# A windowed-attention and top-1 expert kernel: its late expert passes put into the order of the source

## The chip, the cores and the metric

The kernel runs on one core of one Trainium2 chip. The metric is the device time of one execution in microseconds (us), the median of the runs shown. Engines are named as in the profile: PE is TensorE (matmuls; PEld its weight loads), DVE VectorE, ACT ScalarE, POOL GpSimd, SP SyncE, whose queue issues most of the DMAs.

## What is computed

```python
# attention, B=8, H=8, S=576, D=64, causal window of 64
scores = q @ k.T / 8, masked to 0 <= rel < 64
x = softmax(scores) @ v                 # laid out as 4608 rows of 512
# top-1 mixture of 8 experts, D=512, F=1024
logits = x @ w_gate ; e = argmax ; gate = softmax(logits)[e]
out[row] = gate * (relu(x[row] @ w1[e]) @ w2[e])
```

## The kernel before

**Three stages.** A long loop over 36 steps (lines 859 to 932) does the attention of 128 rows a step, stores them in DRAM as `xs` and sorts the rows by expert. In its last steps and after it, four *early* passes (`first_passes`, L822) each take 256 rows of experts 0 to 3. Then `chain` (L967) runs 15 *late* passes: pass 0 and 1 are *wide* (three blocks of 128 rows), passes 2 to 14 are *narrow* (two blocks). Passes beyond these stand behind conditions (L987 to L1000) that do not hold for this input.

**One pass** is `expert` (L290), which walks over eight *slices* j of the 1024 hidden columns. A slice is: the split of the next slice's weights (`split_`, L228: ACT rounds the loaded `raw` to `whi`, L241, DVE forms the rest `wlo`, L238), twelve *up* matmuls into a PSUM bank `hp` (L308 with `whi`, L312 with `wlo`), ACT's `hh` (L318) and DVE's `hl` (L319) from that bank, and then the *down* matmuls of the slice before (`flush`, L279: three a block, of 512 columns), which collect in the banks `yp`. The down matmuls of a pass's slice 7 thus come behind the up matmuls of slice 0 of the next pass. After a pass's last down matmuls ACT scales the rows (`ys`, L267) and POOL scatters them to `out` (L268).

**The weights** of an expert come in four loads of 1 MB (`load`, L210), into the three buffers of `raw`. A split for slices 2r and 2r+1 needs load r; the code asks for load r+1 at the split of slice 2r at the latest. `open_weights` (L812) reads the next pass's expert number into a register of SP and asks for load 0.

**The rows of the next pass** are fetched by POOL (`get`, L774, one indirect DMA a block into one of three buffers `xg`). Pass 0 and the early passes turn them on PE (`turn`, L187: four transposes, an ACT copy L193, a DVE subtraction L194). For passes 1 to 14 four steps do it for each block u: `part` (L786) has DVE separate the two 16-bit halves of each number into `planes` (L790; two buffers) and SP issue a DMA transpose into `halves` (L793; three buffers); `join` (L795) has ACT put the halves together (L799); `lay` (L802) has ACT (L809) and DVE (L810) make the rounded part `xh` and the rest `xl`.

**What sets the order.** Each engine and SP's queue work in order. Within `tc.manual_schedule()` (L857 to L964: the attention and the early passes) the order on each engine is that in which the source issues the instructions. `chain` at L984 stands outside of it: there a planner that estimates costs chooses the order, and it may place instructions of the chain among those of the early passes, as soon as it holds their inputs and buffers to be ready. In the source, `chain` asks for `get(i+2)` after slice 2, `open_weights(i+1)` after slice 4, and for `part`, `join` and `lay` of block u after slices u, 3+u and 4+u.

**The banks.** `turns["yp"]` holds the two halves of one tile `x_b` and two tiles `e_b`, taken in rotation; `t_b` and `m_b` serve `turn`.

Of the kernel before, what the change touches and what calls it, by code (L numbers as in the profile page):

```python
# [14 lines left out]
U16 = mybir.dt.uint16  # L15
# [7 lines left out]
C = H * D  # L23
E, F = 8, 1024
N = B * S
P = 128
# [4 lines left out]
NJ = F // P  # L31
# [16 lines left out]
WIDE = 3  # L48
NWIDE = 2
NARROW = (N // P + E - 1 + E) // 2  # L50
ALWAYS = 13
# [68 lines left out]
def window_attention_then_top1_moe(ctx: ExitStack, tc: tile.TileContext, qkv, wall, wg, cst, out):  # L120
# [13 lines left out]
    t_b = ps.tile([P, C], F32, name="t_b")  # L134
    m_b = ps.tile([P, C], F32, name="m_b")
# [4 lines left out]
    turns = {}  # L140

    def bank(name):

        turns[name].append(turns[name].pop(0))
        return turns[name][-1]
# [38 lines left out]
    def columns(pool, nu=WIDE):  # L184
        return tuple(pool.tile([P, 4, nu * P], F32R, name=n) for n in ("xh", "xl"))
# [12 lines left out]
    class Weights:  # L198


        def __init__(self, ev, spread=0):
            self.ev, self.loaded, self.given, self.raws = ev, 0, 0, {}
            self.first, self.ready, self.spread = None, deque(), spread
            self.load()
# [23 lines left out]
        def split_(self, pieces=None, lows=None):  # L228
            jj, r = divmod(self.given, 2)
            self.given += 1  # L230
            while self.loaded < min(jj + 2, NJ // 2):
                self.load()
            hi = ws.tile([P, 2 * C], F32R, name="whi")
            lo = ws.tile([P, 2 * C], F32R, name="wlo")
            raw = self.raws[jj][:, r]

            def low(s=slice(0, 2 * C)):
                nc.vector.tensor_tensor(out=lo[:, s], in0=raw[:, s], in1=hi[:, s], op=ALU.subtract)  # L238

            def piece(s):  # L240
                nc.scalar.copy(out=hi[:, s], in_=raw[:, s])  # L241
                low(s)

            if lows is not None:
                nc.scalar.copy(out=hi, in_=raw)
                lows.append(low)
            elif pieces is None:
                piece(slice(0, 2 * C))
            else:
                w = 2 * C // 4  # L250
                pieces.extend(lambda s=slice(k * w, (k + 1) * w): piece(s) for k in range(4))
            return hi, lo

    def expert_of(m):
        return nc.sync.value_load(es_sb[m:m + 1, 0:1], min_val=0, max_val=E - 1)
# [3 lines left out]
    def flush(final=False):  # L259

        if not late:
            return
        (hh, hl), yp, (hi, lo), j, last = late.pop()
        def finish(u):
            ix, gate = last[0][u], last[1][u]
            ys = hw.tile([P, C], F32, name="ys")
            nc.scalar.activation(out=ys, in_=yp[u], func=AF.Copy, scale=gate)  # L267
            ins = nc.gpsimd.indirect_dma_start(  # L268
                out=out, out_offset=bass.IndirectOffsetOnAxis(ap=ix, axis=0), in_=ys, in_offset=None,
                bounds_check=N - 1, oob_is_err=False)  # L270

            for o in outs:
                tc.declare_no_dep(ins.ins, o.ins, reason="scatters to rows of their own")
            outs.append(ins)

        for u, y in enumerate(yp):
            us = slice(u * P, (u + 1) * P)
            for m, (x, w) in enumerate(((hh, hi), (hh, lo), (hl, hi))):
                nc.tensor.matmul(y, lhsT=x[:, us], rhs=w[:, C:], start=(j == 0 and m == 0),  # L279
                                 stop=(j == NJ - 1 and m == 2))  # L280
            if final:
                finish(u)
            if u + 1 < len(yp):
                yield
        if last is not None and not final:
            for u in range(len(yp)):
                finish(u)
        yield

    def expert(xt, idx, gates, wts, following=None):  # L290


        xh, xl = xt
        nu = len(idx)
        w = nu * P
        yp = None
        cur = wts.first
        for j in range(NJ):
            if j + 1 < NJ:
                nxt = wts.split()  # L300
            elif following is not None:
                following().first = following().split()
            hi, lo = cur
            hp = bank("hp")
            for kk in range(4):
                ks = slice(kk * P, (kk + 1) * P)
                for x in (xh, xl):
                    nc.tensor.matmul(hp[:, 0:w], lhsT=hi[:, ks], rhs=x[:, kk, 0:w], start=(kk == 0 and x is xh), stop=False)  # L308
                if kk & 1:
                    yield  # L310
            for kk in range(4):
                nc.tensor.matmul(hp[:, 0:w], lhsT=lo[:, kk * P:(kk + 1) * P], rhs=xh[:, kk, 0:w], start=False,  # L312
                                 stop=(kk == 3))
                if kk == 1:
                    yield
            hh = hw.tile([P, WIDE * P], F32R, name="hh")
            hl = hw.tile([P, WIDE * P], F32R, name="hl")
            nc.scalar.activation(out=hh[:, 0:w], in_=hp[:, 0:w], func=AF.Relu)  # L318
            nc.vector.scalar_tensor_tensor(out=hl[:, 0:w], in0=hp[:, 0:w], scalar=0.0, in1=hh[:, 0:w],  # L319
                                           op0=ALU.max, op1=ALU.subtract)  # L320
            yield
            yield from flush()
            if yp is None:
                yp = [bank("yp") for u in range(nu)]
            late.append(((hh, hl), yp, cur, j, (idx, gates) if j == NJ - 1 else None))
            cur = nxt
            yield j
# [439 lines left out]
    passes = [range(WIDE * t, WIDE * (t + 1)) for t in range(NWIDE)]  # L767
    passes += [range(m, m + 2) for m in range(WIDE * NWIDE, NM, 2)]
    xt, wts = {}, {}

    def cols(t, ms):
        return [t[:, m:m + 1] for m in ms]

    def get(i):  # L774
        fetch(xg[i % 3], cols(idx_sb, passes[i]))
# [8 lines left out]
    halves, joined = {}, {}  # L784

    def part(i, u):  # L786
        if u >= len(passes[i]):
            return
        pl = xq.tile([P, 2, C], U16, name="planes")
        nc.vector.tensor_copy(out=pl, in_=xg[i % 3][:, u].bitcast(U16).rearrange("p (f s) -> p s f", s=2))  # L790
        src = pl.rearrange("p s f -> p (s f)")
        halves[i, u] = xq.tile([P, 2 * 4, P], U16, name="halves", bufs=3)
        nc.sync.dma_start_transpose(out=halves[i, u], in_=src)  # L793

    def join(i, u):  # L795
        if u >= len(passes[i]):
            return
        x = joined[i, u] = xq.tile([P, 4, P], F32, name="joined", bufs=3)
        nc.scalar.copy(out=x.rearrange("p k t -> p (k t)").bitcast(U16).rearrange("p (t s) -> p s t", s=2),  # L799
                       in_=halves.pop((i, u)).rearrange("p (s k) t -> p s (k t)", s=2))  # L800

    def lay(i, u):  # L802
        if u >= len(passes[i]):
            return
        if u == 0:
            xt[i] = columns(xw)
        x, us = joined.pop((i, u)), slice(u * P, (u + 1) * P)
        xh, xl = xt[i]
        nc.scalar.copy(out=xh[:, :, us], in_=x)  # L809
        nc.vector.tensor_tensor(out=xl[:, :, us], in0=x, in1=xh[:, :, us], op=ALU.subtract)  # L810

    def open_weights(i):  # L812
        wts[i] = Weights(expert_of(passes[i][0]))

    def each(f, n):
        if 0 <= n < NS:
# [40 lines left out]
    with tc.manual_schedule():  # L857
        keep_busy(BUSY[0])
        for i in range(NS + LAST):
# [36 lines left out]
            if slow and slow[0][0]:  # L896
                f = slow.popleft()[1]
# [41 lines left out]
        xq = ctx.enter_context(tc.tile_pool(name="xq", bufs=2))  # L939
# [27 lines left out]
    def chain(first, last):  # L967
        for i in range(first, last):
            fol = (lambda i=i: wts[i + 1]) if i + 1 < last else None
            for j in expert(xt.pop(i), cols(idx_sb, passes[i]), cols(gate_sb, passes[i]), wts.pop(i), fol):  # L970
                if j == 2 and i + 2 < last:
                    get(i + 2)
                if j == 4 and i + 1 < last:
                    open_weights(i + 1)
                if j in (0, 1, 2) and i + 1 < last:
                    part(i + 1, j)
                if j in (3, 4, 5) and i + 1 < last:
                    join(i + 1, j - 3)
                if j in (4, 5, 6) and i + 1 < last:
                    lay(i + 1, j - 4)  # L980
        for _ in flush(True):
            pass

    chain(0, NWIDE + ALWAYS)  # L984
    total = nc.values_load(tot_sb[0:1, 0:1], min_val=0, max_val=NARROW)
    more = ExitStack()
    for lo, hi in zip(TAIL, TAIL[1:] + [NARROW]):  # L987
# [44 lines left out]
```

## Time and profile before

| what | value |
|---|---|
| median of 3 runs | 654.26 us (653.3 to 655.69) |
| the profiled execution, its own time | 659.39 us |
| its span, first to last instruction | 657.6 us |
| PE busy | 603.9 us (92%) |
| DVE, ACT, POOL busy | 414.4, 391.9, 200.5 us |
| granted TensorE clock, mean | 0.985 of full speed |

The profile page gives busy times by engine, the granted clock and the load of the DMA engines by fortieths of the span, and the chain of work that ended last. Beside it the trace answers questions on a stretch: which instructions ran on an engine, how long the engine sat idle before each (in square brackets, with what ended the idle time), and how busy each engine was. Busy time of PE is no measure of work done at full speed; the granted clock stands beside it.

### The profile page before, as it was taken

To read this page: it belongs to the slowest core of one execution; us is meant where nothing else is said; L and a number is where in the kernel's file an instruction comes from. 1 tells how busy PE (TensorE), PEld (TensorE's weight loads), DVE (VectorE), ACT (ScalarE), POOL (GpSimd) and SP (SyncE) were. 2 spreads that over 40 slices of the span, in tenths; PEclk is the share of its full clock that TensorE was granted. 3 is DMA by queue.
4 is the path that set the end of the run, shared out by engine and by line. 5 is a ranking of instruction groups with operands and counts; after the bars stand their busy time and mean duration, and the time that the engine had idled before them with its cause. 6 is when DMAs were issued, how large, how long until landed. Compare 5 with 4: busy or idle time off the path is not lost.

```text
span 657.6 us, 16869 instructions
## 1 busy us (share of the span) xinstructions
PE 603.9 (92%) x6879; PEld 533.0 (81%) x6879; DVE 414.4 (63%) x736; ACT 391.9 (60%) x792; POOL 200.5 (30%) x180
## 2 busy tenths in 40 slices
PE   8788998788989986995999999999999999999995
PEld 4677877677868975794998889899999999999994
DVE  3666778885699543754454666766666756665551
ACT  4576677675444444661636577667756775776551
POOL 4666667586240343232121232133101110110011
PEclk9999999999999999896999999999999999999999
DMA  8978888843744669797555687788667776565620
GB/s 301 346 257 273 285 262 297 288 154 138 240 152 176 245 224 212 233 218 162 171 193 164 253 261 199 274 278 258 221 219 255 230 235 222 209 215 192 224 98 34
DMA packets 65735, 145.74 MB, mean 222 GB/s; under 512 B 35564, under 2 KB 36716, under 8 KB 56176
## 3 DMA queue, kind: packets, MB, share of 16 engines
q1 hardware_dynamic: 59248, 125.68, 59.2%
q0 software_dynamic: 6400, 18.88, 9.0%
q8 instruction: 56, 0.92, 0.6%
q14 instruction: 31, 0.25, 0.1%
HBM read 119.11 MB, written 19.92 MB: 211 GB/s over the span
## 4 chain that ended last, share of the span: by engine, by line
PE 45%; issue 8%; DMA 6%; DVE 2%; ACT 2%; POOL 1%; POOLq 0%; DVEq 0%; ACTq 0%
PE e_b L308 15%; PE x_b L279 11%; PE e_b L279 11%; PE e_b L312 8%; DMA halves<-planes 5%; DVE wlo L238 1%; DMA xg<-xs,idx_sb 1%; ACT whi L241 1%; POOL out L268 1%; DVE planes L790 1%; ACT joined L799 0%; DVE hl L319 0%; ACT xh L809 0%; ACT ys L267 0%; ACT hh L318 0%
## 5 line engine op out<-in xcount | busy, mean ns | idle before, releaser
L238 DVE TENSOR_TENSOR wlo<-raw,whi 128x1024 fp32r<-128x1024 f32 (+1 forms) x158 | 187.3, 1191 | 102.2 <-ACT whi L241 98.5
L241 ACT CAST whi<-raw 128x1024 fp32r<-128x1024 f32 (+1 forms) x153 | 154.6, 1019 | 97.0 <-PE x_b L279 49.2
L308 PE MATMUL e_b<-xh,whi 128*128 128x256 f32 (+1 forms) x480 | 125.7, 290 | 0.1
L308 PE MATMUL e_b<-xl,whi 128*128 128x256 f32 (+1 forms) x480 | 125.8, 291 | 0.0
L268 POOL DMA_INDIRECT out<-ys,idx_sb x32 | 35.8, 1118 | 280.9 <-ACT ys L267 274.1
L445 POOL TENSOR_TENSOR pm<-tsb,cs 128x512 f32<-128x512 f32 x72 | 90.3, 1275 | 53.1 <-ACT tsb L438 44.9
L318 ACT ACTIVATE hh<-e_b 128x256 fp32r<-128x256 f32 (+1 forms) x152 | 60.3, 397 | 75.1 <-PE e_b L312 72.4
L308 PEld LDWEIGHTS e_b<-xh,whi 128*128 128x128 f32 x480 | 91.3, 190 | 5.3 <-ACT xh L193 0.6
L308 PEld LDWEIGHTS e_b<-xl,whi 128*128 128x128 f32 x480 | 91.2, 190 | 4.9 <-DVE xl L194 0.3
L319 DVE SCALAR_TENSOR_TENSOR hl<-e_b,hh 128x256 fp32r<-128x256 f32 (+1 forms) x152 | 65.8, 433 | 37.4 <-ACT hh L318 35.1
L312 PE MATMUL e_b<-xh,wlo 128*128 128x256 f32 (+1 forms) x480 | 79.9, 288 | 0.0
L279 PE MATMUL e_b<-whi,hl 128*128 128x512 f32 x160 | 63.8, 399 | 11.3 <-DVE hl L319 11.3
L429 ACT ACTIVATE pf<-s_b,mxs 128x64 f32<-128x64 f32 x288 | 62.9, 338 | 10.8 <-DVE mxs L421 8.0
L312 PEld LDWEIGHTS e_b<-xh,wlo 128*128 128x128 f32 x480 | 67.8, 188 | 0.2 <-DVE wlo L238 0.2
L180 POOL DMA_INDIRECT xg<-xs,idx_sb x32 | 42.9, 1342 | 81.7 <-DVE planes L790 33.1
L279 PE MATMUL x_b<-whi,hh 128*128 128x512 f32 x160 | 63.7, 398 | 0.8 <-ACT ys L267 0.8
L459 PE MATMUL x_b<-ring,pm 64*64 64x65 f32 x2176 | 47.0, 222 | 18.7 <-issue 10.8
L279 PE MATMUL x_b<-whi,hl 128*128 128x512 f32 x160 | 63.6, 398 | 0.3 <-DVE hl L319 0.2
L279 PE MATMUL x_b<-wlo,hh 128*128 128x512 f32 x160 | 63.6, 397 | 0.0
L279 PE MATMUL e_b<-wlo,hh 128*128 128x512 f32 x160 | 63.1, 394 | 0.0
L279 PE MATMUL e_b<-whi,hh 128*128 128x512 f32 x160 | 63.0, 394 | 0.0
L459 PEld LDWEIGHTS x_b<-ring,pm 64*64 64x64 f32 x2176 | 41.6, 134 | 24.5 <-issue 16.4
(164 smaller groups left out, 914.4 us busy)
## 6 DMA issues: line engine op xcount, KB each, us to landing
raw<-wall SPq DMA_DIRECT2D x74, 1024.0 KB
ring<-qkv SPq DMA_DIRECT2D x66, 386.0 KB
xs<-xrow SPq DMA_DIRECT2D x36, 256.0 KB
raw<-wall SPq DMA_DIRECT2D x8, 256.0 KB
ring<-qkv SPq DMA_DIRECT2D x4, 256.0 KB
ring<-qkv SPq DMA_DIRECT2D x4, 130.0 KB
ring<-qkv SPq DMA_DIRECT2D x1, 512.0 KB
xg<-xs,idx_sb POOLq DMA_INDIRECT x32
```

The source lines that it names most:

```text
L180: nc.gpsimd.indirect_dma_start(out=t[:, u], out_offset=None, in_=xs[0:rows], in_offset=bass.IndirectOffsetOnAxis(ap=ix, axis=0), bounds_ch ...
L238: nc.vector.tensor_tensor(out=lo[:, s], in0=raw[:, s], in1=hi[:, s], op=ALU.subtract)
L241: nc.scalar.copy(out=hi[:, s], in_=raw[:, s])
L268: ins = nc.gpsimd.indirect_dma_start(out=out, out_offset=bass.IndirectOffsetOnAxis(ap=ix, axis=0), in_=ys, in_offset=None, bounds_check=N ...
L279: nc.tensor.matmul(y, lhsT=x[:, us], rhs=w[:, C:], start=(j == 0 and m == 0), stop=(j == NJ - 1 and m == 2))
L308: nc.tensor.matmul(hp[:, 0:w], lhsT=hi[:, ks], rhs=x[:, kk, 0:w], start=(kk == 0 and x is xh), stop=False)
L312: nc.tensor.matmul(hp[:, 0:w], lhsT=lo[:, kk * P:(kk + 1) * P], rhs=xh[:, kk, 0:w], start=False, stop=(kk == 3))
L318: nc.scalar.activation(out=hh[:, 0:w], in_=hp[:, 0:w], func=AF.Relu)
L319: nc.vector.scalar_tensor_tensor(out=hl[:, 0:w], in0=hp[:, 0:w], scalar=0.0, in1=hh[:, 0:w], op0=ALU.max, op1=ALU.subtract)
L429: nc.scalar.activation(out=pf[:, g, a], in_=sp[:, a, g, 0], func=AF.Exp, bias=mx[:, h:h + 1], scale=SCALE)
L445: nc.gpsimd.tensor_tensor(out=pm[i], in0=t.rearrange("p (g q) -> p g q", g=NG), op=ALU.mult, in1=cc("mask")[:, i * P:(i + 1) * P].unsqueez ...
L459: nc.tensor.matmul(x_b[cols, a, g * V1:(g + 1) * V1], lhsT=pm[i][rows, g, cols], rhs=v_r[rows, c % RING - i, g], start=(i == 0), stop=(i = ...
```

## The change

`chain(0, 15)` moves into a `tc.manual_schedule()` of its own, so that the late passes run in the order of the source. In that order, `part` of the next pass's block u stands after slice u, `join` after slice 3+u (wide pass running) or 4+u (narrow pass running), `lay` one slice behind `join`. `planes` has three buffers instead of two. `open_weights` stands after slice 3 instead of 4, further loads are asked for after slices 4 and 6, and with `far` the split of an odd slice asks for one load more. The last pass takes `t_b` and `m_b` as its banks `yp`.

```diff
-        def __init__(self, ev, spread=0):
+        def __init__(self, ev, spread=0, far=False):
+            self.far = far
...
+            if self.far and r and self.loaded < min(jj + 3, NJ // 2):
+                self.load()
             return hi, lo
...
-        pl = xq.tile([P, 2, C], U16, name="planes")
+        pl = xq.tile([P, 2, C], U16, name="planes", bufs=3)
...
     def open_weights(i):
-        wts[i] = Weights(expert_of(passes[i][0]))
+        wts[i] = Weights(expert_of(passes[i][0]), far=True)
...
     def chain(first, last):
         for i in range(first, last):
             fol = (lambda i=i: wts[i + 1]) if i + 1 < last else None
+            if i + 1 == last:
+                turns["yp"] = [t_b, m_b]
+            gap = 3 if len(passes[i]) == WIDE else 4
             for j in expert(xt.pop(i), cols(idx_sb, passes[i]), cols(gate_sb, passes[i]), wts.pop(i), fol):
+                if j is None or i + 1 == last:
+                    continue
                 if j == 2 and i + 2 < last:
                     get(i + 2)
-                if j == 4 and i + 1 < last:
+                if j == 3:
                     open_weights(i + 1)
-                if j in (0, 1, 2) and i + 1 < last:
-                    part(i + 1, j)
-                if j in (3, 4, 5) and i + 1 < last:
-                    join(i + 1, j - 3)
-                if j in (4, 5, 6) and i + 1 < last:
-                    lay(i + 1, j - 4)
+                if j in (4, 6):
+                    wts[i + 1].load()
+                for f, at in ((part, 0), (join, gap), (lay, gap + 1)):
+                    if 0 <= j - at < len(passes[i + 1]):
+                        f(i + 1, j - at)
         for _ in flush(True):
             pass
 
-    chain(0, NWIDE + ALWAYS)
+    with tc.manual_schedule():
+        chain(0, NWIDE + ALWAYS)
```

## Rows read from the trace of the kernel before

**Rows 1.** Busy time by stretch: window, length, each engine (instructions), clock, DMA share, GB/s.

```profile
241.30:279.60 38.30, 28.22 (x162) 24.00 (x160) 19.58 (x28) 19.99 (x30) 11.10 (x9) 0.91 0.86 228
279.60:321.70 42.10, 34.30 (x161) 30.59 (x162) 19.96 (x26) 16.86 (x23) 10.73 (x8) 0.88 0.77 175
321.70:355.00 33.30, 33.30 (x171) 30.14 (x169) 16.67 (x21) 17.27 (x24) 6.10 (x5) 1.00 0.56 183
355.00:625.80 270.80, 270.42 (x1733) 245.38 (x1732) 173.43 (x231) 183.13 (x260) 43.44 (x35) 1.00 0.71 233
```

**Rows 2.** Waits of PE from 241 to 322: total us, times, longest.

```profile
PE e_b L279 <- DVE hl L319: 10.4, 2, 7.8
PE e_b L312 <- DVE wlo L238: 5.7, 2, 3.1
```

**Rows 3.** Chain that ended last, 225 to 312: start, us, what.

```profile
249.69 12.74 DMA halves<-planes
...
288.29 13.81 DMA halves<-planes
```

**Rows 4.** DVE in order of time: start, us, instruction, idle time before it.

```profile
244.83 0.69 DVE L790 COPY planes<-xg 128x1024 uint16<-128x1024 uint16 x1 [4.74 <-DMA xg<-xs,idx_sb]
...
262.53 0.69 DVE L790 COPY planes<-xg 128x1024 uint16<-128x1024 uint16 x1 [7.29 <-DMA halves<-planes]
```

**Rows 5.** PE in order of time: first up matmul of passes, one down matmul.

```profile
217.56 0.39 PE L279 MATMUL x_b<-whi,hl 128*128 128x512 f32 x1
217.79 0.28 PE L308 MATMUL e_b<-xeh,whi 128*128 128x256 f32 x1
...
241.26 0.28 PE L308 MATMUL e_b<-xeh,whi 128*128 128x256 f32 x1
...
279.62 0.44 PE L308 MATMUL e_b<-xh,whi 128*128 128x384 f32 x1
...
321.55 0.34 PE L308 MATMUL e_b<-xh,whi 128*128 128x384 f32 x1
...
354.88 0.28 PE L308 MATMUL e_b<-xh,whi 128*128 128x256 f32 x1
...
625.75 0.28 PE L308 MATMUL e_b<-xh,whi 128*128 128x256 f32 x1
```

**Rows 6.** All engines in order of time around one block turned on PE.

```profile
271.21 0.60 PE L191 MATMUL m_b<-cs,xg 128*128 128x128 f32 x4
271.57 0.36 PE L308 MATMUL e_b<-xeh,whi 128*128 128x256 f32 x1
...
272.46 0.69 DVE L194 TENSOR_TENSOR xl<-m_b,xh 128x512 fp32r<-128x512 f32 x1 [1.61 <-ACT xh L193]
```

**Rows 7.** Chain that ended last, whole span: start, us, what.

```profile
403.91 4.57 DMA halves<-planes
...
452.31 0.95 PE e_b L308 x8
...
474.71 0.95 PE e_b L308 x8
```

**Rows 8.** Groups from 290 on: count, busy us, mean ns, idle us before.

```profile
L241 ACT CAST whi<-raw 128x1024 fp32r<-128x1024 f32 x115 | 120.0, 1054 | 92.7 <-PE x_b L279 49.2 <-PE e_b L279 41.0 <-DMA raw<-wall 1.2
...
L318 ACT ACTIVATE hh<-e_b 128x256 fp32r<-128x256 f32 x104 | 40.1, 386 | 30.9 <-PE e_b L312 30.4 <-issue 0.4
...
L799 ACT COPY joined<-halves 128x1024 uint16<-128x1024 uint16 x23 | 31.3, 1362 | 0.5 <-DVE xl L810 0.5
...
L809 ACT CAST xh<-joined 128x512 fp32r<-128x512 f32 x26 | 14.7, 618 | 0.0
```

**Rows 9.** All engines in order of time at the end of the kernel.

```profile
649.77 0.50 PE L279 MATMUL x_b<-whi,hh 128*128 128x512 f32 x1 [0.78 <-ACT ys L267]
...
649.99 0.98 POOL L268 DMA_INDIRECT out<-ys,idx_sb  x1 [18.68 <-ACT ys L267]
...
651.74 0.98 POOL L268 DMA_INDIRECT out<-ys,idx_sb  x1 [0.77 <-ACT ys L267]
```

More of the change, by code (lines that the diff above doesn't have):

```diff
@@ L786, in part @@
     def part(i, u):
-        if u >= len(passes[i]):
-            return
-        pl = xq.tile([P, 2, C], U16, name="planes")
+        pl = xq.tile([P, 2, C], U16, name="planes", bufs=3)
         nc.vector.tensor_copy(out=pl, in_=xg[i % 3][:, u].bitcast(U16).rearrange("p (f s) -> p s f", s=2))
@@ L795, in join @@
     def join(i, u):
-        if u >= len(passes[i]):
-            return
         x = joined[i, u] = xq.tile([P, 4, P], F32, name="joined", bufs=3)
@@ L802, in lay @@
     def lay(i, u):
-        if u >= len(passes[i]):
-            return
         if u == 0:
```

## The prediction

> **What bounds the kernel now.** I read first where PE, the busiest engine, is not busy in the late part, then what it waits for there, then the engine that it waits for. The table of stretches [rows 1] splits the late part at the starts of passes. From 355.0 to 625.8 us (twelve narrow passes) PE is busy for 270.42 of 270.80 us at full clock; the wide pass 1 before it, 321.7 to 355.0, has no idle time at all. There nothing but fewer matmuls would help. The two stretches ahead are different: 28.22 busy of 38.30 us in the last early pass, 34.30 of 42.10 in late pass 0, and the granted clock is 0.91 and 0.88 on average, so at the lower of its two levels (1.2 instead of 2.4 GHz) for part of both. So the loss is local: it lies between 241 and 322 us.
>
> PE's waits there [rows 2] are for DVE: 10.4 us for `hl`, 5.7 us for `wlo`. These two are short instructions; the question is what DVE did instead. DVE's own order [rows 4] shows it: a `planes` copy of 0.69 us stands idle 4.74 us at 244.83, until the fetched rows land, and another 7.29 us until 262.53, for a DMA transpose to free one of two `planes` buffers. `planes` belongs to the chain, yet 244.83 lies in the last early pass, which begins at 241.26 and ends with the first up matmul of pass 0 at 279.62 [rows 5]. So the planner outside of the manual region has put work of the next pass into DVE's in-order queue ahead of work that PE needs at once. The chain of waits says the same: two transposes of 12.74 and 13.81 us stand on it [rows 3]. In the steady part the one long transpose of the chain took 4.57 us [rows 7].
>
> **Part 1: the order of the source, 241 to 322 us.** With the chain in a manual region, no `part` can come ahead of the early passes' instructions on DVE, nor a `join` on ACT. What the stretch should then take comes from neighbours that run without such work. The early pass before (217.79 to 241.26) took 23.47 us with two blocks turned; the last one turns three, and a turn takes PE 0.36 us (271.21 to 271.57) [rows 6]: 23.83 us. Wide pass 1 took 33.33 us (321.55 to 354.88) [rows 5]; pass 0 is like it, but its first down matmuls are those of a two-block pass, six instead of nine at 0.23 us (217.56 to 217.79): 32.64 us. Together 56.5 us, against 80.3 us (241.26 to 321.55): 23.8 us to gain, some 14.5 in the early pass (38.36 less 23.83) and 9.3 in pass 0.
>
> The new order also costs something here. The third block of pass 0 is turned behind the last slice of the early pass, and in the source the next PE instruction is the up matmul that needs the result; the six down matmuls that could hide it come later. From the start of a turn to the end of DVE's `xl` it was 1.94 us (271.21 to 273.15), of which PE works 0.36 [rows 6]. So up to 1.6 us of stall, nothing if a planner-like overlap remained; the source leaves none, so I take 1.5. Net 22.3 us.
>
> **Part 2: the steady passes.** PE cannot go faster, so the question is whether the new order holds it up. ACT has 1.05 for `whi` and 0.39 for `hh` in each slice, and in the fullest slice of a narrow pass also a `join` of 1.36 and an `xh` of 0.62 [rows 8]: 3.42 us against a slice of 2.80 us (22.40 from pass to pass, 452.31 to 474.71, by eight) [rows 7]. The slices around it need 2.80 and 2.06, so the excess of 0.6 is made up in the next one, and the hidden part is possible because a slice's down matmuls come behind the next slice's up matmuls, 2.8 us after `hh` can start. I cost it at nothing; without that cover it would be 0.6 us a narrow pass, 8 us in all. The two scaled outputs `ys` come at a slice without `join` and are left where they are. What can still be gained: 270.87 us (354.88 to 625.75) stand against 12 times 22.40 and 0.69 for the first pass's wide down matmuls, 269.5. Between 0 and 1.4 us; the traces name no cause that the change removes, so 0.
>
> **Part 3: DMAs and SP's queue.** Moved with the order are the transposes (3 for pass 1, 2 for each later pass), the fetches and the weight loads. A transpose now is issued behind slice u and needed four narrow slices later, 11.2 us (12.5 in a wide pass). The steady one took 4.57 us, so it is hidden, and the third `planes` buffer takes away the wait of DVE seen in [rows 4]. In SP's queue the load asked for after slice 2's split stands behind the second transpose, and the loads after slices 3, 4 and 6 wait for buffers whose last readers are splits already issued; behind each waits only the next load or transpose. ACT waited 1.2 us in all for a weight load in the passes from 290 on [rows 8], which is the only sign of a late load. Cost between 0 and 1.2 us a narrow pass, nearest to 0 because SP was that far ahead before; 0 taken. The register read in `open_weights` moves one slice earlier on SP alone: nothing.
>
> On the transposes a rule stands against the first part. The row: 12.74 and 13.81 us where fetches were issued beside them, 4.57 in the steady stretch [rows 3, 7]. The Trainium skill ("DMA: Bandwidth & Descriptors", section "Queues, rings and completion order") says that each DMA engine takes turns, packet by packet, between the queue rows that have work, so a transpose beside a fetch is slow wherever the source puts it. By that rule pass 0, which has three transposes, the scatters of the early pass and the fetch of pass 2, could keep its loss; that is the second rival below.
>
> **Part 4: the last pass's banks.** Its last three down matmuls stood idle 0.78 us for `ys` of the other half of the same tile [rows 9]; with separate tiles they do not. POOL issues the second scatter at 651.74, and the first keeps it to 650.97, so at most 0.77 us reach the end; I take 0.5. Nothing else of the tail moves.
>
> **The sum.** 22.3 + 0 + 0 + 0.5 = 22.8 us; with all bounds on the good side 25.7 (23.8 + 1.4 + 0.5), and 17 if loads or ACT's order take a few us. The profiled execution took 659.39 us, 5.1 more than the median of 654.26. On the profiled one the sum gives 636.6, on the median 631.5. If those 5.1 us lie in the very transposes that go (tracing may slow them), the median gains only 17.7 and the time is 636.5; that end stays in the range.
>
> **Rivals.**
> *Slower: late transposes stall ACT in every pass.* ACT works in order, so a `join` whose transpose has not landed holds up `whi` and `hh`. The new order issues transposes later than the planner did. At 13.81 us [rows 3] one is 2.6 us late against 11.2, and ACT has no slack to hide it (part 2), so 13 narrow passes lose 34 us, the sum turns to a loss of 11 and the time to 665. It decides from 22.8 over 13, 1.75 us a pass, that is from transposes of 13.0 us. For it: two of that length were seen. Against it: in the steady stretch scatters ran beside them as well and the chain has 4.57. The Trainium skill ("DMA: Bandwidth & Descriptors", "Rules for kernel authors") advises to issue a DMA early and to wait for it late, which speaks for this rival; the row of 4.57 does not bear it out.
>
> *Only half: pass 0 keeps its loss.* Its transposes have 12.5 us; if they take 13 to 14 and the slices pile up as before, the 9.3 us stay and the gain is 14.5 − 1.5 + 0.5 = 13.5: 640.8.
>
> *Weights late.* The odd load behind the transposes costs ACT 1.2 us in each of 13 passes, 15.6: gain 7, time 647.
>
> *No change.* The loss moves on: the rows for pass 1 come from the same fetches, and the transposes still meet the loads; PE waits as long, only later. 654. Against it: the queue order, not the DMA, made PE wait in [rows 4].
>
> **How the numbers follow.** Forecast (22.8, or 17.7 with the tracing's share) 0.70; half 0.12; weights late 0.06; no change 0.04; slower 0.08. The range from 627 to 642 holds the first two, 0.82. A measurement tells about 0.5% (3.3 us) from no change; all of the first three are beyond that: faster 0.88, same 0.04, slower 0.08.
>
> **What would show it.** Right: no `planes` before the last early pass is over, 23 to 24 us for that pass and some 34 for pass 0, the clock at 1.00 in both, 22.4 us a narrow pass as before, one PE gap of 1 to 1.6 us ahead of pass 0. Wrong: PE waits for `whi`, `hh` or `wlo` in every narrow pass with ACT idle ahead of `joined` (slower), or ahead of `whi` for `raw` (weights); or pass 0 over 40 us (half).

## The result: 20 us less, and where they were

The changed kernel's median is 635.04 us (632.17 to 637.3, four runs) beside 654.98 us (653.3 to 657.89) for the kernel before in the same comparison: a ratio of 0.9689, interval 0.9635 to 0.9742. The forecast was 631.5, with a range from 627 to 642. Here and below a median is that of all runs; a ratio and its interval leave out the few runs that were over 1.5% slower than the fastest of their kernel. The profiled execution of the changed kernel took 632.17 us, span 630.3 us, mean granted clock 0.993; the one of before took 659.39, span 657.6.

The first view of the profile after is the busy time of each engine over the span.

```profile
PE 599.6 (95%) x6879; PEld 531.9 (84%) x6879; DVE 415.3 (66%) x736; ACT 386.2 (61%) x792; POOL 203.3 (32%) x180
```

PE is busy 4.3 us less than before with the same matmuls; the rest of the 27.3 us between the two spans is idle time of PE that went. The second view is the table of stretches, cut at the starts of the last early pass, late pass 0, pass 1 and the narrow passes, as in [rows 1] (columns: window, length, PE, PEld, DVE, ACT and POOL busy with their instructions, clock, DMA share, GB/s).

```profile
236.50:261.20 24.70, 24.02 (x158) 21.57 (x156) 14.85 (x19) 13.62 (x22) 3.02 (x3) 1.00 0.68 251
261.20:294.80 33.60, 33.02 (x165) 29.73 (x166) 18.04 (x25) 17.80 (x24) 4.72 (x4) 1.00 0.58 181
294.80:328.10 33.30, 33.30 (x169) 30.17 (x168) 16.59 (x21) 16.97 (x23) 6.53 (x5) 1.00 0.54 176
328.10:598.50 270.40, 270.39 (x1732) 246.09 (x1731) 179.74 (x240) 183.34 (x265) 64.57 (x47) 1.00 0.74 247
```

Against [rows 1] the last early pass is shorter by 13.6 us and pass 0 by 8.5, and in both the clock stands at 1.00 instead of 0.91 and 0.88. DVE has 19 instructions in the last early pass where it had 28: the chain's work is gone from there. By the same two rows, 16.6 of these 22.1 us are idle time of PE (17.9 before, 1.3 after), and 5.5 are matmuls that were busy for longer (62.5 against 57.0). Pass 1 and the twelve narrow passes are as they were. What PE still waits for shows in the starts of pass 0 (start, busy us, engine, line, operation, and in brackets the idle time with what ended it):

```profile
261.19 0.44 PE L311 MATMUL e_b<-xh,whi 128*128 128x384 f32 x1 [0.68 <-ACT xh L193]
262.22 0.44 PE L311 MATMUL e_b<-xl,whi 128*128 128x384 f32 x1 [0.58 <-DVE xl L194]
```

These are the two halves of the stall for the third turned block. The 10.4 us for `hl` and the 5.7 for `wlo` of [rows 2] have gone to 0.2 and 0.4, from 200 us to the end (first two rows), and the first `planes` copy stands in pass 0, no longer in the early pass [rows 4] (third row, from DVE in order of time):

```profile
PE e_b L315 <- DVE wlo L239: 0.4, 1, 0.4
PE x_b L282 <- DVE hl L322: 0.2, 1, 0.2
...
265.43 0.68 DVE L791 COPY planes<-xg 128x1024 uint16<-128x1024 uint16 x1
```

The late part, from the start of the last early pass to the issue of the last scatter, took 410.48 us before (241.26 to 651.74) and takes 387.55 after (236.49 to 624.04): 22.9 us less, where the sum had 22.8. The other 4.8 us between the two profiles lie ahead of the first early pass, in attention code that the change leaves alone: that pass begins at 155.2 us in the profile of before, at 150.3 in this one, and between 151.0 and 154.5 in the twelve further kernels below.

### The profile page after: what moved, and what is told of

Its sections match the earlier page's. It is cut to its first block, busy times and chain, and to the rows that moved or that the text cites. A ratio compares the mean times of both kernels' runs of the same rounds, so it can differ in the third digit from the quotient of the medians.

```text
span 630.3 us, 16808 instructions
## 1 busy us (share of the span) xinstructions
PE 599.6 (95%) x6879; PEld 531.9 (84%) x6879; DVE 415.3 (66%) x736; ACT 386.2 (61%) x792; POOL 203.3 (32%) x180
## 4 chain that ended last, share of the span: by engine, by line
PE 72%; DVE 10%; issue 9%; POOL 4%; DMA 2%; ACT 2%; SPq 0%; POOLq 0%; ACTq 0%; DVEq 0%
PE e_b L311 21%; PE x_b L282 15%; PE e_b L282 15%; PE e_b L315 10%; PE x_b L462 3%; POOL pm L448 2%; PE s_b L405 2%; PE m_b L479 2%; DVE wlo L239 2%; DVE s_b L422 1%; DVE s_b L416 1%; DMA ring<-qkv 1%; DVE xrow L472 1%; PE m_b L523 1%; POOL out L271 1%
## 5 line engine op out<-in xcount | busy, mean ns | idle before, releaser
L271 POOL DMA_INDIRECT out<-ys,idx_sb x32 | 41.8, 1307 | 270.2 <-ACT ys L270 265.7
L432 ACT ACTIVATE pf<-s_b,mxs 128x64 f32<-128x64 f32 x288 | 63.1, 339 | 10.6 <-DVE mxs L424 8.6
L282 PE MATMUL x_b<-whi,hl 128*128 128x512 f32 x144 | 56.5, 392 | 0.2 <-DVE hl L322 0.2
L282 PE MATMUL x_b<-wlo,hh 128*128 128x512 f32 x144 | 56.6, 393 | 0.0
L282 PE MATMUL x_b<-whi,hh 128*128 128x512 f32 x144 | 56.5, 392 | 0.0
```

The lines of the kernel that those rows point to most:

```text
L271: ins = nc.gpsimd.indirect_dma_start(out=out, out_offset=bass.IndirectOffsetOnAxis(ap=ix, axis=0), in_=ys, in_offset=None, bounds_check=N ...
L432: nc.scalar.activation(out=pf[:, g, a], in_=sp[:, a, g, 0], func=AF.Exp, bias=mx[:, h:h + 1], scale=SCALE)
```

## The experiments

The kernels are the changed one with one edit, unless something else is said. "Narrow pass" is the mean of passes 2 to 13, by the starts of their first up matmuls.

**The changed kernel again**, to measure the gain itself.

> The changed kernel once more, unaltered, timed in five rounds against the kernel before, to place the gain between two readings. Theory (the gain is what the late part shows, 22.9 us from the start of the last early pass to the last scatter): a difference of 22 to 24 us in the medians, and a second profile with the last early pass at 24.7 us and late pass 0 at 33.6 us, whatever the attention part does. Rival (tracing lengthened the transposes of the kernel before, so an untraced run gains less): a difference of 17 to 19 us. In both, the start of the first early pass, 150.3 us here and 155.2 us before, should come out elsewhere again if it is chance, and at 150 again if the change has moved it.

It took 635.51 us (633.82 to 639.42) against 654.75 (649.59 to 659.74, seventeen runs), ratio 0.9716 (0.9664 to 0.9768): 19.2 us between these medians, and by the ratio a gain of 18.6 us with ends of about 15 and 22. The last early pass took 24.70 us again and pass 0 33.62. The interval holds both 17.7 and, just, 22; it does not tell the two apart.

**The order taken back.** All other edits stay; the planner chooses the chain's order again.

```diff
-    with tc.manual_schedule():
-        chain(0, NWIDE + ALWAYS)
+    chain(0, NWIDE + ALWAYS)
```

> The changed kernel with the chain taken out of the manual region again; all other edits stay (third planes buffer, slices of part, join and lay, weights asked for sooner, own banks). Theory (the planner's order of the in-order queues made the loss): the loss comes back, last early pass and pass 0 together about 80 us instead of 58.3, time within 4 us of the kernel before (650 to 656). Rival (the third planes buffer and the sooner weights made most of the gain): 60 to 68 us for the two passes, time 633 to 642.

661.26 us (656.93 to 666.92), ratio 1.0104 (1.0067 to 1.0141): the loss is back, and a little more. The stretches of this kernel (columns as above), and the waits of PE and DVE there (total us, times, longest):

```profile
240.10:280.30 40.20, 30.26 (x163) 25.71 (x162) 19.62 (x28) 20.07 (x30) 10.30 (x9) 0.83 0.92 220
280.30:322.60 42.30, 33.81 (x161) 30.08 (x162) 20.36 (x27) 16.68 (x23) 10.30 (x9) 0.88 0.80 180
```

```profile
PE e_b L282 <- DVE hl L322: 10.6, 2, 8.5
DVE planes L791 <- DMA halves<-planes: 15.7, 6, 7.9
```

The 10.6 us for `hl` answer to the 10.4 of [rows 2]. DVE still stands 15.7 us for transposes, though `planes` now has three buffers; it was 22.2 us from 241 to 322 in the kernel before, and the two passes are no shorter for the difference. So the order alone brings the two passes from 82.5 to 58.3 us, and the third buffer doesn't.

**The order alone**, on the kernel before: two buffers, the weights asked for as before, rotating banks.

```diff
-    chain(0, NWIDE + ALWAYS)
+    with tc.manual_schedule():
+        chain(0, NWIDE + ALWAYS)
```

> The kernel before with one edit: the chain stands in a manual region. Two planes buffers, join three slices behind part everywhere, weights opened after slice 4 and each later load asked for one split ahead, shared banks. Theory (the order alone gives the gain): last early pass and pass 0 together 58 us, narrow passes 22.4 us, time 632 to 637. Rival (in the source's order the weights come too late, so the sooner loads are needed): ACT waits for raw, 1 to 3 us in each of 14 passes, narrow passes 23.5 to 25.5 us, time 646 to 675.

671.85 us (669.52 to 674.58), ratio 1.0249 (1.0179 to 1.0318). The two passes are cured, 24.70 and 33.61 us; the narrow ones are not left alone, they take 23.6 to 30.5 us, 25.97 in the mean. The table of stretches, the waits of ACT and PE, and pieces of the chain that ended last (start, us, what) of this kernel:

```profile
237.90:262.60 24.70, 24.02 (x158) 21.58 (x156) 14.91 (x19) 13.79 (x22) 3.02 (x3) 1.00 0.55 208
...
329.50:641.10 311.60, 285.89 (x1732) 251.38 (x1731) 179.00 (x240) 182.98 (x265) 62.91 (x47) 0.97 0.71 219
```

```profile
ACT whi L241 <- DMA raw<-wall: 58.2, 23, 5.3
PE e_b L308 <- ACT whi L241: 25.0, 17, 4.1
```

```profile
363.12 1.28 SPq L793
364.65 7.95 DMA raw<-wall
372.62 1.05 ACT whi L241
...
395.27 9.47 DMA raw<-wall
404.76 1.05 ACT whi L241
...
405.86 1.22 PE e_b L308 x8
```

The chain reads downward: SP's queue issues a transpose, the weight load behind it takes 7.95 us, ACT splits it at last, PE goes on. Of the 41 us that the twelve passes lost, 25.7 are idle time of PE (311.60 less 285.89). The other 15.5 are the same 1732 matmuls being busy for longer (285.89 against 270.39). The granted clock is only a part of that. Its mean is 0.97 because it stood at the lower level in four stretches, 17.05 us in all, each in or just behind one of the four longest waits (2.25 to 4.13 us); the first of them, cut where the clock changes:

```profile
353.61:357.02 3.41, 3.41 (x12) 2.69 (x11) 3.15 (x6) 1.99 (x3) 0.00 (x0) 0.50 0.41 173
```

In the four PE was busy for 15.38 us with 61 matmuls, which at the changed kernel's rate (270.39 us for 1732) would take 9.5: an estimate of some 6 us for the clock. The rest, some 0.5 us a wait, is lost next to the waits at the full clock too: eight up matmuls took 1.22 us behind the wait that ended at 405.86, and 0.95 in the steady passes [rows 7]. Why, no run here shows. The planner, with the same source, had kept ACT's wait for weights at 1.2 us [rows 8]. What the change gains is then not the order alone, but the order with the loads placed anew for it.

**Weights asked for as before**, in the new order.

```diff
-        wts[i] = Weights(expert_of(passes[i][0]), far=True)
+        wts[i] = Weights(expert_of(passes[i][0]), far=False)
...
-                if j == 3:
+                if j == 4:
                     open_weights(i + 1)
-                if j in (4, 6):
-                    wts[i + 1].load()
```

> The changed kernel with the sooner weights undone alone (opened after slice 4, no loads after slices 4 and 6, no load ahead at odd splits); manual region, gaps, third planes buffer and own banks stay. Theory (order_only was slow because its loads were issued behind the transposes and fetches of slices 0 to 2 and landed in 7 to 10 us): the same loss as there, narrow passes 24 to 28 us, time 655 to 675, with ACT idle for raw. Rival (order_only was slow because join stood three slices behind part and planes had two buffers): narrow passes 22.4 to 22.9 us, time 634 to 640.

674.28 us (672.16 to 676.87) against 655.92, ratio 1.027 (1.0238 to 1.0302); a narrow pass takes 25.88 us. ACT's and PE's waits in this kernel, and SP's queue in one narrow pass:

```profile
ACT whi L242 <- DMA raw<-wall: 66.0, 21, 6.0
PE e_b L311 <- ACT whi L242: 24.0, 17, 4.6
```

```profile
443.68 1.28 SPq L794 DMA_TRANSPOSE halves<-planes  x1
445.20 0.38 SPq L224 DMA_DIRECT2D raw<-wall  x1
447.43 1.48 SPq L794 DMA_TRANSPOSE halves<-planes  x1
449.15 7.03 SPq L224 DMA_DIRECT2D raw<-wall  x3
```

By the source, two of a pass's four loads are issued in the pass before; the third stands between the two transposes here, the fourth behind the second one. ACT waits for just these two (two rows of ACT in order of time):

```profile
452.05 1.04 ACT L242 CAST whi<-raw 128x1024 fp32r<-128x1024 f32 x1 [3.85 <-DMA raw<-wall]
...
460.27 1.04 ACT L242 CAST whi<-raw 128x1024 fp32r<-128x1024 f32 x1 [3.46 <-DMA raw<-wall]
```

The next two kernels each undo one half.

**Without `far`** (`far=False` alone).

> The changed kernel without the load ahead at odd splits; next pass's loads stay after slices 3, 4 and 6. Only the last load of a pass moves, from slice 2 to slice 5, one split ahead of its use. Theory (any load that is issued less than its landing time of 5 us ahead of its split stalls ACT): the last load has one split, 2.8 us, and ACT waits some 2 to 3 us in every narrow pass, of which PE sees 1 to 3: time 647 to 670. Rival (with the DMA engines free in slice 5 the load is back in time for the cover of 2.8 us): 634 to 640.

634.41 us (633.85 to 635.04), ratio 0.967 (0.9646 to 0.9694); a narrow pass takes 22.50 us, and ACT's waits for weights sum to 2.7 us over seven places. In one point the expectation was wrong in itself: without `far` the last load is asked for at the split of slice 4, one slice later than with it and two splits ahead of its use, not in slice 5. The last early pass took 25.62 us in this kernel, 0.9 more than in the changed kernel; ACT waited 3.5 us for weights there.

**With `far`, without the rest**: the next pass's weights opened after slice 4, none asked for after slices 4 and 6.

```diff
-                if j == 3:
+                if j == 4:
                     open_weights(i + 1)
-                if j in (4, 6):
-                    wts[i + 1].load()
```

> The changed kernel with the load ahead at odd splits kept, but the next pass opened after slice 4 and nothing asked for after slices 4 and 6. Then the next pass's second load is issued at its first split and the third one at slice 0, among the transposes, scatters and fetches. Theory: these loads land late as in order_only (7 to 10 us), ACT waits, narrow passes 23.5 to 26 us, time 648 to 672. Rival (the load at odd splits alone is enough): 634 to 640.

633.36 us (631.94 to 635.27), ratio 0.9666 (0.9632 to 0.9699); a narrow pass takes 22.49 us, ACT's waits for weights sum to 1.4. So either half alone is enough, and without both the kernel is 39 us slower. What the two have in common shows in SP's queue, of the kernel without `far` (three rows) and of this one (two rows):

```profile
442.49 0.33 SPq L224 DMA_DIRECT2D raw<-wall  x1
447.92 5.60 SPq L794 DMA_TRANSPOSE halves<-planes  x2
453.76 11.46 SPq L224 DMA_DIRECT2D raw<-wall  x4
```

```profile
461.69 0.33 SPq L224 DMA_DIRECT2D raw<-wall  x1
467.22 4.98 SPq L794 DMA_TRANSPOSE halves<-planes  x2
```

The third load of the pass is issued 5.4 and 5.5 us ahead of the pass's first transpose; in the kernel with both halves undone it stands behind that transpose. A load issued in the quiet stretch is what keeps ACT fed while the transposes, the scatters and the fetch are under way. That this one load is the whole of it is read from the two queues and was not tried by itself.

**The join one slice behind the part**, which takes the slack of the transposes from 11.2 us to 2.8.

```diff
-            gap = 3 if len(passes[i]) == WIDE else 4
+            gap = 1
```

> The changed kernel with join one slice behind part in every pass (instead of three or four). A transpose then has 2.8 us in a narrow pass, against a median of 5.1 us from issue to landing in the changed kernel, so it is some 2.3 us late or more. This prices the slower rival of the prediction. As priced there (no slack on ACT): each pass loses the lateness of two transposes, 2.3 to 4.6 us, time 665 to 695. Theory (a slice of slack: hh is needed 2.8 us after it can start, whi one slice ahead): PE loses 0 to 1 us a pass, time 635 to 648.

678.09 us (672.04 to 681.27), ratio 1.0355 (1.0319 to 1.0391); a narrow pass takes 25.57 us. ACT's and PE's waits, and the stretch of the twelve narrow passes:

```profile
ACT joined L798 <- DMA halves<-planes: 36.8, 24, 3.7
PE e_b L311 <- ACT whi L242: 21.9, 17, 3.3
```

```profile
331.40:638.20 306.80, 285.14 (x1732) 248.03 (x1732) 181.67 (x240) 183.80 (x265) 60.92 (x47) 0.99 0.67 220
```

A join that waits 1.5 us (36.8 over 24) two times a pass goes with a pass that is 3.0 us longer: ACT, working in order, passes the wait on to `whi` and so to PE. It does not pass on all of it. PE stands idle for 21.7 us (306.80 less 285.14), so ACT's slack hides some 15 of the 36.8; but the matmuls are busy for 14.8 us more than in the changed kernel, as in the order alone, and that gives it back. My theory, that ACT's slack hides the wait, falls with that. The pricing of the slower rival in the prediction came out right in the sum, by luck, since the two cancel; its condition, transposes of over 13 us, is not met. The 5.1 us that I had gone by is no good median: the first profile of the changed kernel tells the landing of three of its 29 transposes. The second one tells that of 26; their median is 3.5 us, against 3.4 here, and the longest took 5.9.

The Trainium skill ("DMA: Bandwidth & Descriptors", "Rules for kernel authors") advises to issue a DMA early, compute, and wait for it late; the 3.0 us that a pass loses here agree.

**The third block turned one slice sooner** (the three `flip` of pass 0 after slices 4, 5 and 6 of the last early pass).

```diff
-            if e == EARLY - 1 and j == NJ - 3:
+            if e == EARLY - 1 and j == NJ - 4:
...
-            if e == EARLY - 1 and j is not None and j >= NJ - 3:
-                flip(0, [j - NJ + 3])
+            if e == EARLY - 1 and j is not None and NJ - 4 <= j < NJ - 1:
+                flip(0, [j - NJ + 4])
```

> The changed kernel with the three blocks of pass 0 turned after slices 4, 5 and 6 of the last early pass instead of 5, 6 and 7. Theory (PE stands for 1.3 us, 0.68 and 0.58, ahead of pass 0 because the third block is turned right ahead of the matmuls that read it): both gaps go, last early pass and pass 0 together 57.0 us instead of 58.3, 1.3 us less, within the noise of the time but plain in the profile. Rival (the stall only moves, since the fetched rows or ACT's queue are late one slice sooner): the same 58.3 us or more, with a wait of the transposes for xg.

634.54 us (631.71 to 635.22), ratio 0.9685 (0.9636 to 0.9734). The two passes of this kernel, by stretch:

```profile
238.20:262.00 23.80, 23.80 (x157) 21.60 (x156) 14.30 (x18) 13.39 (x22) 3.02 (x3) 1.00 0.66 242
262.00:294.70 32.70, 32.70 (x167) 29.66 (x166) 18.77 (x25) 17.94 (x25) 4.73 (x4) 1.00 0.65 199
```

PE has no idle time left, and by the starts the passes take 23.86 and 32.65 us, 56.51 in sum: the 56.5 that the prediction had put together from their neighbours. The profile shows the 1.8 us; the times (634.5 beside 635.0 and 635.5) are too close to show them.

**Some of the planner's hoisting put back by hand**: `get(2)` and the three `part` of pass 1 behind slice 0 of the last early pass, once with two buffers of `planes` and once with three.

```diff
+            if e == EARLY - 1 and j == 0:
+                get(2)
+                for u in range(WIDE):
+                    part(1, u)
```

> The changed kernel, all in the order of the source, with what the planner did put back by hand: the fetch of pass 2 and all three parts of pass 1 stand behind slice 0 of the last early pass, and planes has two buffers again. Theory (DVE and SP work in order, so a planes copy that waits for rows or for a buffer holds up wlo and hl, and the transposes hold up the weight loads behind them): the last early pass grows from 24.7 us by 4 to 12 us, with DVE idle ahead of planes and PE idle for DVE or for whi. Rival (the planner's loss came from its order elsewhere, in ACT's or PE's queue): 24.7 to 26 us. Late pass 0 stays at 33.6 us in both, as its parts are done.

> As hoist2, with three planes buffers. If DVE's wait for a free buffer is what costs, this has only the wait for the fetched rows left: last early pass 24.7 to 28 us. If the place in the queues costs whatever the buffers are (SP's transposes ahead of the weight loads, beside the fetch), it grows as in hoist2, by 4 to 12 us.

Profiled, it took 641.93 us with two buffers and 642.84 with three, beside 657.4 for before (single executions). The last early pass grew by 8.2 and by 8.9 us, pass 0 stayed at 33.60, and the clock of the early pass fell to 0.90 in both. With two buffers it is DVE that is held (DVE in order of time, and PE's wait):

```profile
247.88 0.69 DVE L791 COPY planes<-xg 128x1024 uint16<-128x1024 uint16 x1 [5.59 <-DMA halves<-planes]
248.49 1.22 DVE L239 TENSOR_TENSOR wlo<-raw,whi 128x1024 fp32r<-128x1024 f32 x1
```

```profile
PE e_b L315 <- DVE wlo L239: 5.7, 1, 5.7
```

With three buffers DVE's wait for a buffer is gone and PE waits as long, now for ACT, which waits for a weight load:

```profile
254.80 1.04 ACT L242 CAST whi<-raw 128x1024 fp32r<-128x1024 f32 x1 [8.82 <-DMA raw<-wall]
```

```profile
PE e_b L311 <- ACT whi L242: 6.2, 1, 6.2
```

That the queue holds the load back shows in SP's rows, of the changed kernel (first) and of this one:

```profile
237.91 6.34 SPq L224 DMA_DIRECT2D raw<-wall  x2
```

```profile
247.90 11.03 SPq L224 DMA_DIRECT2D raw<-wall  x3
```

The first load of the last early pass is issued 1.4 us after the start of that pass there (236.49), and 9.9 us after it here (238.04), behind the three transposes; it then takes 6.9 us to land.

So early transposes block twice: in DVE's queue, behind a buffer, and in SP's, where the load stands behind them and beside the fetch. Taking away the first wait uncovers the second, at the same price.

**Two buffers of `planes`, nothing else changed** (`bufs=3` removed).

> The changed kernel with two planes buffers. In the source's order a part is followed by the next one a slice later and its transpose has landed two slices on (5.1 us against 5.6 in a narrow pass, 8.3 in a wide one). Theory: no DVE wait worth telling, the two passes 58.3 us and narrow ones 22.4 to 22.6 us, no change. Rival (the third buffer is needed): DVE waits ahead of planes, over 60 us or narrow passes over 23 us.

632.56 us (a single execution); 24.70 and 33.60 us for the two passes, 22.52 for a narrow one. In the new order the third buffer does nothing.

**The last pass on the rotating banks** (the line that gives it `t_b` and `m_b` removed).

> The changed kernel with the last pass on the rotating banks as before. From the first up matmul of pass 14 to the issue of the last scatter it was 25.99 us before and 25.54 in the changed kernel. Theory (the halves of one tile make PE wait for ys): 0.78 us of PE idle ahead of the last three down matmuls again, and 25.9 to 26.1 us. Rival (the saving came from the order of the instructions): 25.5 us.

634.07 us (a single execution). The end of the changed kernel (two rows), then of this one (three):

```profile
622.76 0.98 POOL L271 DMA_INDIRECT out<-ys,idx_sb  x1 [18.69 <-ACT ys L270]
624.04 0.98 POOL L271 DMA_INDIRECT out<-ys,idx_sb  x1 [0.30 <-DVEq L1003]
```

```profile
624.48 0.50 PE L282 MATMUL x_b<-whi,hh 128*128 128x512 f32 x1 [0.78 <-ACT ys L270]
624.70 0.98 POOL L271 DMA_INDIRECT out<-ys,idx_sb  x1 [18.69 <-ACT ys L270]
626.46 0.98 POOL L271 DMA_INDIRECT out<-ys,idx_sb  x1 [0.78 <-ACT ys L270]
```

PE's 0.78 us of [rows 9] is back, and the scatters are issued 1.76 us apart instead of 1.28; from the start of pass 14 to the last scatter it is 26.0 us against 25.5. But from the last scatter to the end of the span it is 5.7 to 5.8 us in the three kernels with shared banks whose end was read (this one, before, the order alone) and 5.8 to 6.9 in the eleven with banks of their own. The scatter comes half a us earlier and lands about as much later, so at the end next to nothing is left. From its issue to its landing the last scatter took 3.4 to 3.6 us in those three and 3.5 to 4.6 in the eleven.

## Why the prediction held, point by point

**The place and the cause** were right. The loss was local, between 241 and 322 us; taking the order back brings it back (82.5 us), and the order alone cures it (58.31). That the planner had put work of the chain ahead of the early pass's in the queues is what both hoisted kernels reproduce, each with over 8 of the early pass's 13.6 us. Pass 0's share of 8.5 us was not put back by hand; that it belongs to the planner's order rests on the kernel with the order taken back.

**Part 1** was right in each term: 56.5 us by the neighbours, 56.51 where the last stall is gone; a stall of 1.5 us taken, 0.68 and 0.58 measured in brackets, 1.8 by the lengths of the passes; 58.0 predicted for both, 58.31 measured.

**Part 2**, nothing for the steady passes: 22.57 us before, 22.53 after.

**Part 3** gave the right sum by an argument that was partly wrong, so that its 0 was in part luck. It took the loads as hidden because SP "was that far ahead before". It was the planner that had put SP that far ahead, and the source's order alone loses it: 3.4 us a narrow pass, nearly three times the 1.2 us of the upper bound. That bound came from a wait of before, which shows what late loads cost in the planner's order, not in the new one. The cost was 0 only because the change also asks sooner, which the prediction listed among the moves and didn't price. The rival "weights late" had the mechanism and less than half of its size: 15.6 us against the 40 that twelve passes lost with the loads late. The third buffer, which was to take away DVE's wait, does nothing in the new order, and in the planner's the two passes are no shorter with it.

**"The queue order, not the DMA, made PE wait"**: right, with more queues than the prediction looked at. It had DVE's; SP's would have cost the same by itself, as the kernel with three buffers shows. The Trainium skill's rule on queue rows taking turns ("DMA: Bandwidth & Descriptors", "Queues, rings and completion order") had spoken for the rival in which pass 0 keeps its loss. Pass 0, with its transposes, the scatters and a fetch, has 0.58 us of idle time behind its start, and the clock at 1.00. The rule may hold of each transfer, which no run here tests; in this order PE waits for none of them.

**Part 4** was sized right at the scatter, 0.5 us, and the prediction ended there. It said that nothing else of the tail moves, and the last landing does, later by about as much, so the term belongs at about 0.

**The sum and the median.** 22.8 us forecast for the late part and 22.9 measured in the profiles, but 19.9 and 19.2 between the medians. The forecast for the median, 631.5, lies 3.5 below 635.04. Some 3 of the 5.1 us by which the profile of before exceeds its median are accounted for: attention in that execution took 155.2 us where the middle of the other thirteen profiles is 152.0, and chance in attention isn't a gain of the change. That leaves some 2 us for which the late part of the profiled execution may have been longer than usual, by tracing or by chance. Whether it was is open: only one execution of before was profiled, and the intervals of the medians are wider than that.

## What to carry to other kernels

Where the busiest engine waits for a short instruction of another engine, look at what stood ahead of that instruction in its in-order queue, and which part of the program it came from; a scheduler that hoists work because its inputs look ready can put a wait for a DMA there. Whoever then fixes the order by hand takes over the placing of the loads too: price every load and transpose by what stands ahead of it in the issuing queue, because here the order alone was 17 us slower than the planner's and the order with the loads moved 20 us faster. Asking early helps what is issued, and hurts whatever urgent stands behind it in the same queue, by 8.9 us for the one load behind three early transposes.

## What the runs showed of the hardware that was not expected

A weight load of 1 MB has no fixed time to land: the median was 6.2 us in the second execution of the changed kernel and 7.5 in the one with its loads behind the transposes, with 7.95 and 9.47 us on the chain of the order alone. This is from issue to landing, so a wait behind other transfers is in it. (The first profile of the changed kernel tells the landing of only ten loads.)

```profile
raw<-wall SPq DMA_DIRECT2D x74, 1024.0 KB, 6.2
```

Waits of PE cost more than their length: in the order alone, with 25.7 us of idle time, most of it in 17 waits of up to 4.1 us, the matmuls of twelve passes were also busy for 15.5 us more, of which an estimated 6 us go with the lower clock and the rest with the waits at the full clock. With the late joins it was 14.8 us beside 21.7 of idle time, at a mean clock of 0.99. And two scatters issued closer together land later: the half a us gained at the issue of the second was about lost behind it.
